# Decode attention, forward and backward: dK blocks alternate with the next pair's K blocks, and two V blocks take the place of dK blocks behind the sum of exponents

## The chip, the cores and the metric

The kernel runs on one core of a Trainium2 chip. Its engines work in parallel, each through its own queue in order: PE (TensorE, matmuls and transposes through the identity), DVE (VectorE), ACT (ScalarE), POOL (GpSimd) and SP (SyncE), which here issues the large transfers. The metric is the device time of one execution in microseconds. Before the change the median of three runs is 634.05 us (633.49 to 634.83).

## The reference

One query row per head, 32 heads, 8192 keys of 128 numbers, bf16. The kernel returns the attention output and the gradients of all three inputs:

```python
B, H, Sq, Skv, Dh = 1, 32, 1, 8192, 128
scores = jnp.einsum('bhqd,bhkd->bhqk', q, k) * Dh ** -0.5
attn = softmax(scores, axis=-1)                    # p
out = jnp.einsum('bhqk,bhkd->bhqd', attn, v)
# backward, for a given grad_out (do):
# dV = p (outer) do;  dp = V do;  ds = p * (dp - sum(p * dp)) * scale
# dK = ds (outer) q;  dq = ds K
```

K and V are read once (134 MB in all), and dK and dV, which are as large, are written once.

## The kernel before

Heads go in pairs: HP = 16 pairs, and the loop over t from 1 to 16 (L468) takes one pair a turn (pair 0 is done by `first()`; turn 16 only finishes). A pair's K and V are 4 MB each and lie in SBUF as 128 partitions by 128 rows by 128 numbers. There are three buffers for K and two for V. dK is written over K and dV over V, in place, and stored from there, so the load of pair t+2 waits until the store from the same buffer has landed.

The order of each engine's work is written out by hand (`tc.manual_schedule`, L100): an engine takes its instructions in the order of the Python calls. The work of a pair is cut in NB = 8 blocks of 16 rows:

- `k_block` (L197): DVE transposes a K block into one of three buffers named XK (L200), and PE adds four matmuls of it into the scores' bank `s_ps` (L208). XK is shared with the V blocks.
- `s_back`, `s_top` (L212, L217): DVE brings the scores back (`sT`, L215), takes the maximum, and PE spreads it (L223). `s_exp` (L225): DVE makes `nbias` (L230), ACT the exponents `e` and their sums (L233). `s_sum` (L237): PE adds the sums (L238).
- `p_of` (L247): DVE takes the reciprocal (L250); ACT makes `p_rep` (L252) and `win_p`, the weights for PE (L244).
- The V side. In turns 3 to 14 (`wide`, L257) half of V is transposed by DVE in four V blocks (`v_block`, L295, at L298), each read by four matmuls (`v_wide`, L302, at L310) into `dp_ps`. The other half goes through PE transposes (`v_part`: L273, copied by ACT at L279) and small matmuls (`v_scores`, L290). In the other turns all of V goes that second way.
- `contract` (L342): PE's products with V (`acc_p`) and, later, with K (`acc_ds`), both at L349. The first needs `win_p`, the second `win_ds`.
- `outer` (L367): DVE writes one block of dV (`"p"`) or dK (`"ds"`), at L371. `dk(a, b)` inside the loop does dK blocks a to b-1 of the pair in front, o = t-1, and issues the store of that dK when its last block (in the last two pairs: each half) is done.
- `v_back`, `pd_sum`, `ds_of` (L316 to L340): `dp_ps` comes back as `dpT` (L319), is multiplied and summed, and ds is made; ACT makes `win_ds` and `ds_rep`, which the dK blocks read.

A turn of 3 to 14 before the change goes, on DVE: dK blocks 0 to 3 of pair t-1; `sT`, maximum; dK block 4; `nbias`; dK blocks 5 and 6; reciprocal; V blocks 0 to 3; dK block 7; dV blocks 0 to 6 of pair t; `dpT`; dV block 7; ds; and the eight K blocks of pair t+1 in a row. On PE: the maximum's transpose, the sum, then four rounds of one `v_wide`, a quarter of `contract` for p and two `v_part`s, then `v_scores`, `contract` for ds, and the matmuls of the K blocks. SP's queue holds, turn by turn: the store of dK, the store of dV, the load of K, the load of V.

Of the kernel before, what the change touches and what calls it, by code (L numbers as in the profile page):

```python
# [15 lines left out]
NB = 8  # L16
# [11 lines left out]
def kernel(  # L28
# [14 lines left out]
    HP = H // 2  # L43
# [22 lines left out]
    psQ = ctx.enter_context(tc.tile_pool(name="psQ", bufs=1, space=PSUM))  # L66
    psM = ctx.enter_context(tc.tile_pool(name="psM", bufs=1, space=PSUM))

    st, acc = {}, {}
    k_in = [consts.tile([P, NT, D], BF16, name=f"K{i}") for i in range(K_BUFS)]  # L70
    v_in = [consts.tile([P, NT, D], BF16, name=f"V{i}") for i in range(V_BUFS)]
    Kt = {t: k_in[t % K_BUFS] for t in range(HP)}
# [2 lines left out]
    def rows_of(x, t, a, b):  # L75
        return x[0, 2 * t:2 * t + 2].rearrange("h s d -> (h s) d").rearrange("(p n) d -> p n d", p=P)[:, a:b, :]
# [120 lines left out]
    def k_block(t, c):  # L197
        x = st.setdefault(t, {})
        X = xkpool.tile([P, BN, NW, QD], F32, tag="XK", name="XK_sb")
        nc.vector.transpose(X[:], Kt[t][:, c * BN:(c + 1) * BN, :].rearrange("p n d -> p (n d)").bitcast(F32).rearrange(  # L200
            "p (n w j) -> p n w j", n=BN, w=NW))
        if c == 0:
            x["s"] = psS.tile([P, 512], F32, tag="s", name="s_ps")
        cols = X[:].rearrange("p n w i -> p (n w i)").bitcast(BF16).rearrange(
            "p (n w i e) -> p w e n i", n=BN, w=NW, e=2)
        for w in range(NW):
            for e2 in range(2):
                nc.tensor.matmul(x["s"][:], lhsT=q_win[:, 2 * w + e2, SL - 1 - c:SL - 1 - c + P],  # L208
                                 rhs=cols[:, w, e2], start=(c == 0 and w == 0 and e2 == 0),
                                 stop=(c == NB - 1 and w == NW - 1 and e2 == 1), skip_group_check=True)  # L210
# [6 lines left out]
    def s_top(t):  # L217
        x = st[t]
        mx = small.tile([P, 1], F32, tag="mx")
        nc.vector.reduce_max(mx[:], x["sT"][:, :, 0:NB], axis=AX.XY)  # L220
        top = small.tile([P, 1], F32, tag="top")
        nc.vector.tensor_scalar_mul(top[:], mx[:], scale)  # L222
        nc.tensor.transpose(x["m"][:, 128:256], top[:].to_broadcast([P, P]), ident_f[:])  # L223
# [13 lines left out]
    def s_sum(t, rs):  # L237
        nc.tensor.matmul(st[t]["m"][:, 0:1], lhsT=same[:], rhs=rs[:], start=True, stop=True, skip_group_check=True)  # L238
# [18 lines left out]
    def wide(t):  # L257
        return 3 <= t < HP - 1
# [22 lines left out]
    def v_scores(t, z):  # L281
        x = st[t]
        cols = x.pop(("XV", z)).rearrange("p m s -> p (m s)").bitcast(BF16).rearrange(
            "p (m s e) -> p e m s", s=P, e=2)
        if z == 0 and not wide(t):
            x["dp"] = psD.tile([P, 512], F32, tag="dp", name="dp_ps")
        at = SL - 2 - 2 * z
        for e2 in range(2):
            for b in range(NQ):
                nc.tensor.matmul(x["dp"][b * QD:(b + 1) * QD, :], lhsT=do_win[:, b // 2, e2, at:at + QD],  # L290
                                 rhs=cols[:, e2, :, b * QD:(b + 1) * QD],
                                 start=(not wide(t) and z == 0 and e2 == 0),
                                 stop=(z == (1 if wide(t) else NZ - 1) and e2 == 1), skip_group_check=True)

    def v_block(t, r):  # L295

        X = xkpool.tile([P, NM, NW, QD], F32, tag="XK", name="XV_blk")
        nc.vector.transpose(X[:], Vt[t][:].rearrange("p n d -> p (n d)").bitcast(F32).rearrange(  # L298
            "p (m r w j) -> p m r w j", r=SL, w=NW, j=QD)[:, :, SL // 2 + r])
        st[t]["XW", r] = X  # L300
# [66 lines left out]
    def outer(t, which, r):  # L367
        x = st[t]
        X, row = (Kt[t], 0) if which == "ds" else (Vt[t], 1)
        a, b = r * BN, (r + 1) * BN  # L370
        nc.vector.tensor_tensor(  # L371
            X[:, a:b, :].rearrange("p n (a b) -> p n a b", b=R),
            x[which][:, a:b, :].unsqueeze(2).to_broadcast([P, BN, D // R, R]),
            x["qd"][:, row, :].rearrange("p (a b) -> p a b", b=R).unsqueeze(1).to_broadcast([P, BN, D // R, R]),
            op=ALU.mult)

    def store(t, which, parts=1, last=None):
        X, dst = (Kt[t], out_2) if which == "ds" else (Vt[t], out_3)
        L = NT // parts
        for c in (range(parts) if last is None else (last,)):  # L380
            nc.sync.dma_start(rows_of(dst, t, c * L, (c + 1) * L), X[:, c * L:(c + 1) * L, :])
# [86 lines left out]
    for t in range(1, HP + 1):  # L468
        o = t - 1
        now = t < HP  # L470
        parts = 2 if o >= HP - 2 else 1

        def dk(a, b):
            for r in range(a, b):
                outer(o, "ds", r)
                if (r + 1) % (NB // parts) == 0:
                    store(o, "ds", parts, r * parts // NB)

        blocks = now and wide(t)
        if blocks:  # L480

            dk(0, 4)
            s_back(t)
            s_top(t)
            dk(4, 5)
            rs = s_exp(t)
            s_sum(t, rs)
            dk(5, NB - 1)
            p_of(t)
            for r in range(3):  # L490
                v_block(t, r)
            for i in range(4):
                v_wide(t, i)
                if i == 0:
                    v_block(t, 3)
                    dk(NB - 1, NB)
                contract(t, "p", i * NG // 4, (i + 1) * NG // 4)
                for z in range(2):
                    v_part(t, z * (NM // TB) + i)
                if i == 3:  # L500
                    for z in range(2):
                        v_scores(t, z)
                outer(t, "p", 2 * i)
                if i < 3:
                    outer(t, "p", 2 * i + 1)
            weights_do(t + 1)
            if wide(t + 1):
                weights_wide(t + 1)
        else:
            dk(0, 3)  # L510
            if now:
                v_part(t, 3)
                v_part(t, 4)
                s_back(t)
                s_top(t)
                v_scores(t, 0)
                v_part(t, 5)
                v_part(t, 6)
                rs = s_exp(t)
                for m in (7, 8, 9):  # L520
                    v_bank(t, m)
                s_sum(t, rs)
                v_copy(t, 7)
                v_copy(t, 8)
            dk(3, 4)
            if now:
                p_of(t)
                v_copy(t, 9)
                v_scores(t, 1)
                v_part(t, 10)  # L530
                v_part(t, 11)
                contract(t, "p")
                v_part(t, 12)
                v_part(t, 13)
                v_scores(t, 2)
                v_part(t, 14)
                v_part(t, 15)
                v_scores(t, 3)
                if t + 1 < HP:
                    weights_do(t + 1)  # L540
                    if wide(t + 1):
                        weights_wide(t + 1)
        if not now:
            dk(4, NB - 1)
            results()
            dk(NB - 1, NB)
            break
        fine, early = t == HP - 1, NB - 1 if blocks else 2
        if not blocks:
            dk(4, NB)  # L550
            outer(t, "p", 0)
            outer(t, "p", 1)
            if fine:
                store(t, "p", 4, 0)
        v_back(t)
        pd_sum(t)
        if t % ST == 0:
            gather(o, "ds")
        outer(t, "p", early)
        if blocks:  # L560
            store(t, "p")
        ds_of(t)
        contract(t, "ds")
        if t % ST == ST - 1:
            gather(t, "p")
        if t + 1 < HP:
            prepare(t + 1)
        else:
            gather(t, "ds")
        done = 0  # L570
        for r in range(early + 1, NB):
            outer(t, "p", r)
            if fine and r % 2:
                store(t, "p", 4, r // 2)
            if t + 1 < HP and t != 1:
                k_block(t + 1, done)
                done += 1
        if not fine and not blocks:
            store(t, "p")
        if t + 1 < HP:  # L580
            for c in range(done, NB):
                k_block(t + 1, c)
                if not wide(t + 1) and c > HALF:
                    v_part(t + 1, c - HALF - 1)
        if t + 2 < HP:
            weights_q(t + 2)
            load_k(t + 2)
            load_v(t + 2)
# [32 lines left out]
```

## Time and profile before

| | before |
|---|---|
| median of three runs | 634.05 us |
| the profiled execution | 634.35 us |
| its span | 632.5 us |
| mean granted clock of PE | 0.812 |
| busy: PE, DVE, ACT | 426.6, 550.5, 176.2 us |
| DMA, share of 16 engines, rate | 99.0%, 425 GB/s |
| DVE waiting for PE before a K block | 37.9 us |

The profile shows one execution. L200 is line 200 of the kernel, "DVE" or "PE" the engine. In the slices a digit is the busy share in tenths of one fortieth of the span, for PEclk the clock that PE was granted in tenths of full. The chain goes back from the last instruction to whatever released it, step by step, and gives shares of the span. A line of the waits reads: who waited <- for whom: microseconds in total, times, longest. In the order of time a line gives start, duration, engine, line, operation, tiles and, in brackets, the idle time before it and who ended it. In a table of stretches a line gives the stretch, its length, the busy time of PE, PE's weight loads, DVE, ACT and POOL with the number of instructions, the granted clock, the DMA share and GB/s.

### The profile page before, as it was taken

The page shows a single profiled execution, that of the slowest core. Times are in us where ns is not written, and L with a number is a line of the kernel's source. Part 1 is how long each engine was busy: PE and PEld are TensorE (multiplying, and loading weights), DVE is VectorE, ACT ScalarE, POOL GpSimd, SP SyncE. Part 2 cuts the span into 40 slices and gives each one's busy share as a digit, 9 for nine tenths or more (in the row PEclk, how much of TensorE's full clock was granted, in tenths as well). Part 3 has the DMA queues.
Part 4 walks back from the last instruction along what each step waited for, and adds up shares of the span by engine and source line. Part 5 has one row for each costly group of instructions (what it writes and reads, how often), then busy time and mean ns, then how long its engine had stood idle before and what let it go on. Part 6 is the DMA issues. An engine that isn't in the chain of part 4 may idle for free.

```text
span 632.5 us, 7251 instructions
## 1 busy us (share of the span) xinstructions
PE 426.6 (67%) x2876; PEld 207.7 (33%) x2876; DVE 550.5 (87%) x630; ACT 176.2 (28%) x439; POOL 9.2 (1%) x27
## 2 busy tenths in 40 slices
PE   5868686488475874758747587474875748757870
PEld 2635252144242421323323242231332314223540
DVE  8688987997988979899797997989979799798893
ACT  1616152041240322404124031240412304122530
POOL 2000000000000000000000000000000000000000
PEclk9989697787698776888868877687886878768965
DMA  8999999999999999999999999999999999999997
GB/s 361 434 418 433 431 430 430 433 432 430 431 430 430 434 424 435 428 435 432 434 443 430 429 432 432 428 431 432 431 428 431 430 431 432 430 432 432 411 407 310
DMA packets 11025, 268.92 MB, mean 425 GB/s; under 512 B 1392, under 2 KB 1392, under 8 KB 1392
## 3 DMA queue, kind: packets, MB, share of 16 engines
q1 hardware_dynamic: 10896, 268.46, 99.0%
q8 instruction: 22, 0.36, 0.2%
q14 instruction: 11, 0.09, 0.0%
q10 hardware_dynamic: 96, 0.02, 0.0%
HBM read 134.23 MB, written 134.23 MB: 424 GB/s over the span
## 4 chain that ended last, share of the span: by engine, by line
PE 41%; DVE 40%; issue 7%; ACT 6%; DMA 4%; DVEq 0%; ACTq 0%
DVE K L371 18%; PE T_ps L273 9%; PE dp_ps L310 9%; DVE XK_sb L200 9%; PE acc_ds L349 7%; PE acc_p L349 6%; PE s_ps L208 5%; DVE V L371 5%; DMA K<-in_k_dram 3%; PE dp_ps L290 3%; DVE XV_blk L298 2%; ACT XV_sb L279 2%; ACT win_ds L244 2%; DVE sT L215 2%; DVE dpT L319 1%
## 5 line engine op out<-in xcount | busy, mean ns | idle before, releaser
L200 DVE STREAM_TRANSPOSE XK_sb<-K 128x1024 f32<-128x1024 f32 x128 | 148.6, 1215 | 40.3 <-PE s_ps L208 37.9
L371 DVE TENSOR_TENSOR V<-p_rep,qd 128x2048 bf16<-128x2048 bf16 x128 | 150.8, 1219 | 7.6 <-PE T_ps L273 3.4
L371 DVE TENSOR_TENSOR K<-ds_rep,qd 128x2048 bf16<-128x2048 bf16 x128 | 149.2, 1211 | 0.5
L208 PE MATMUL s_ps<-XK_sb,q_win 128*128 128x512 bf16 x512 | 132.9, 404 | 9.9 <-DVE XK_sb L200 5.8
L279 ACT COPY XV_sb<-T_ps 128x512 f32<-128x512 f32 x144 | 78.2, 589 | 130.4 <-PE T_ps L273 130.3
L273 PE MATMUL T_ps<-ident_f,V 128*128 128x128 f32 x640 | 92.8, 293 | 0.1
L273 PEld LDWEIGHTS T_ps<-ident_f,V 128*128 128x128 f32 x640 | 75.3, 150 | 34.0 <-issue 26.6
L310 PE MATMUL dp_ps<-XV_blk,do_wide 128*128 128x512 bf16 x192 | 62.3, 454 | 31.2 <-DVE XV_blk L298 31.2
L208 PEld LDWEIGHTS <-q_win 128*128 128x128 bf16 x512 | 50.9, 102 | 85.0 <-issue 38.3
L349 PE MATMUL acc_ds<-K,win_ds 128*32 128x512 bf16 x512 | 52.9, 586 | 33.3 <-ACT win_ds L244 33.3
L298 DVE STREAM_TRANSPOSE XV_blk<-V 128x1024 f32<-128x1024 f32 x48 | 55.3, 1208 | 0.0
L223 PE MATMUL m_ps<-ident_f,top 128*128 128x128 f32 x16 | 6.7, 416 | 62.2 <-DVE top L222 62.2
L349 PE MATMUL acc_p<-V,win_p 128*32 128x512 bf16 x512 | 42.7, 428 | 1.6 <-ACT win_p L244 1.6
L310 PEld LDWEIGHTS <-do_wide 128*128 128x128 bf16 x192 | 19.9, 109 | 49.6 <-DVE XV_blk L298 32.2
L349 PEld LDWEIGHTS <-win_ds 128*32 128x32 bf16 x512 | 17.2, 130 | 56.1 <-ACT win_ds L244 31.2
L185 ACT COPY q_win<-q_blk 128x16 bf16<-128x16 bf16 x16 | 4.2, 261 | 108.7 <-PE s_ps L208 108.7
L233 ACT ACTIVATE e<-sT,nbias 128x128 f32<-128x128 f32 x16 | 8.2, 515 | 69.7 <-DVE nbias L230 69.7
L223 PEld LDWEIGHTS m_ps<-ident_f,top 128*128 128x128 f32 x16 | 2.7, 170 | 68.8 <-issue 62.2
L290 PE MATMUL dp_ps<-XV_sb,do_win 128*32 128x512 bf16 x288 | 20.8, 383 | 5.2 <-ACT XV_sb L279 5.0
L238 PE MATMUL m_ps<-rs,same 128*128 128x1 f32 x32 | 8.3, 327 | 18.1 <-ACT e L233 18.1
L244 ACT ACTIVATE win_ds<-ds,rinv_s 64x128 bf16<-64x128 f32 x32 | 12.8, 399 | 27.5 <-DVE ds L336 27.3
L328 PE MATMUL m_ps<-pd,same 128*128 128x1 f32 x32 | 6.1, 260 | 19.8 <-DVE m_ps L322 19.8
(68 smaller groups left out, 215.0 us busy)
## 6 DMA issues: line engine op xcount, KB each, us to landing
K<-in_k_dram SPq DMA_DIRECT2D x15, 4096.0 KB, 19.2
V<-in_v_dram SPq DMA_DIRECT2D x15, 4096.0 KB, 19.3
out_dram<-V SPq DMA_DIRECT2D x15, 4096.0 KB, 25.4
out_dram<-K SPq DMA_DIRECT2D x14, 4096.0 KB, 27.4
out_dram<-K SPq DMA_DIRECT2D x4, 2048.0 KB, 9.5
K<-in_k_dram SPq DMA_DIRECT2D x4, 1024.0 KB, 8.2
V<-in_v_dram SPq DMA_DIRECT2D x4, 1024.0 KB, 15.6
out_dram<-V SPq DMA_DIRECT2D x4, 1024.0 KB, 8.3
```

The costliest lines, as they stand in the source:

```text
L200: nc.vector.transpose(X[:], Kt[t][:, c * BN:(c + 1) * BN, :].rearrange("p n d -> p (n d)").bitcast(F32).rearrange("p (n w j) -> p n w j", ...
L208: nc.tensor.matmul(x["s"][:], lhsT=q_win[:, 2 * w + e2, SL - 1 - c:SL - 1 - c + P], rhs=cols[:, w, e2], start=(c == 0 and w == 0 and e2 == 0),
L215: nc.vector.transpose(x["sT"][:].rearrange("p n r -> p (n r)"), x.pop("s")[:])
L223: nc.tensor.transpose(x["m"][:, 128:256], top[:].to_broadcast([P, P]), ident_f[:])
L244: nc.scalar.activation(win[which][a:b, :, at + 4 * s:at + 4 * s + 4], src[a:b].rearrange("p (g j) -> p g j", j=4), ACT.Copy, scale=1.0 if ...
L273: nc.tensor.transpose(T_ps[:, j, :], words[:, at * P:(at + 1) * P], ident_f[:])
L279: nc.scalar.copy(x["XV", z][:, i * TB:(i + 1) * TB, :], x.pop(("T", m))[:])
L290: nc.tensor.matmul(x["dp"][b * QD:(b + 1) * QD, :], lhsT=do_win[:, b // 2, e2, at:at + QD], rhs=cols[:, e2, :, b * QD:(b + 1) * QD], start ...
L298: nc.vector.transpose(X[:], Vt[t][:].rearrange("p n d -> p (n d)").bitcast(F32).rearrange("p (m r w j) -> p m r w j", r=SL, w=NW, j=QD)[:, ...
L310: nc.tensor.matmul(st[t]["dp"][:], lhsT=do_wide[:, 2 * w + e2, at:at + P], rhs=cols[:, w, e2], start=(r == 0 and w == 0 and e2 == 0), stop ...
L349: nc.tensor.matmul(acc[which][b * QD:(b + 1) * QD, :], lhsT=win[which][:, g, at:at + QD], rhs=X[:, 4 * g:4 * g + 4, :].rearrange("p n d -> ...
L371: nc.vector.tensor_tensor(X[:, a:b, :].rearrange("p n (a b) -> p n a b", b=R), x[which][:, a:b, :].unsqueeze(2).to_broadcast([P, BN, D // ...
```

## The change

`dk` now takes only the block up to which to go, and remembers in `wrote` how far the pair's dK is written, so a pair's dK blocks can be begun in the turn before. In the turns of 3 to 14, dK blocks 0 to 3 of pair t (0 to 2 in turn 14) are placed behind K blocks 2 to 5 (2 to 4) of pair t+1. In the next turn dK blocks 4 and 5 stand ahead of `sT`, block 6 behind the maximum, and behind `nbias` and the sum come V blocks 0 and 1, where dK blocks 5 and 6 were; then the reciprocal and `p_of`, V blocks 2 and 3, and dK block 7 as before. Turn 3 has no dK block placed ahead and writes six before `sT`. In turn 15 dK block 3, with the store of the first half, stands behind the maximum, and block 4 ahead of the reciprocal; three more follow it. Nothing changes in what is computed, nor in the order of PE, ACT, POOL and SP.

```diff
-    st, acc = {}, {}
+    st, acc, wrote = {}, {}, {}
...
-        parts = 2 if o >= HP - 2 else 1
-
-        def dk(a, b):
-            for r in range(a, b):
+
+        def dk(b, o=o):
+
+            parts = 2 if o >= HP - 2 else 1
+            for r in range(wrote.get(o, 0), b):
                 outer(o, "ds", r)
                 if (r + 1) % (NB // parts) == 0:
                     store(o, "ds", parts, r * parts // NB)
+                wrote[o] = r + 1
...
-            dk(0, 4)
+            dk(6)
             s_back(t)
             s_top(t)
-            dk(4, 5)
+            dk(NB - 1)
             rs = s_exp(t)
             s_sum(t, rs)
-            dk(5, NB - 1)
+            v_block(t, 0)
+            v_block(t, 1)
             p_of(t)
-            for r in range(3):
-                v_block(t, r)
+            v_block(t, 2)
             for i in range(4):
                 v_wide(t, i)
                 if i == 0:
                     v_block(t, 3)
-                    dk(NB - 1, NB)
+                    dk(NB)
...
-            dk(0, 3)
+            dk(3)
             if now:
                 v_part(t, 3)
                 v_part(t, 4)
                 s_back(t)
                 s_top(t)
+                if t == HP - 1:
+                    dk(4)
                 v_scores(t, 0)
...
-            dk(3, 4)
+            dk(5 if t == HP - 1 else 4)
...
-            dk(4, NB - 1)
+            dk(NB - 1)
             results()
-            dk(NB - 1, NB)
+            dk(NB)
...
             for c in range(done, NB):
                 k_block(t + 1, c)
+                if blocks and 2 <= c < (6 if wide(t + 1) else 5):
+                    dk(c - 1, t)
                 if not wide(t + 1) and c > HALF:
                     v_part(t + 1, c - HALF - 1)
```

More of the change, by code (lines that the diff above doesn't have):

```diff
@@ L549 @@
         if not blocks:
-            dk(4, NB)
+            dk(NB)
             outer(t, "p", 0)
```

## The prediction

> **What bounds the kernel now.** I read the page first (share of the engines, the slices, the queues, the chain), then the waits, then one middle turn in order of time, then the granted clock in stretches.
>
> ```profile
> span 632.5 us, 7251 instructions
> ...
> PE 426.6 (67%) x2876; PEld 207.7 (33%) x2876; DVE 550.5 (87%) x630; ACT 176.2 (28%) x439; POOL 9.2 (1%) x27
> ...
> PEclk9989697787698776888868877687886878768965
> DMA  8999999999999999999999999999999999999997
> ...
> q1 hardware_dynamic: 10896, 268.46, 99.0%
> ...
> PE 41%; DVE 40%; issue 7%; ACT 6%; DMA 4%; DVEq 0%; ACTq 0%
> ```
>
> Two things could set the pace. The DMA engines are full in nearly every slice. Yet the chain that ended last holds 4% of DMA and is a relay of PE and DVE. The waits decide between them:
>
> ```profile
> DVE XK_sb L200 <- PE s_ps L208: 37.9, 17, 4.6
> ...
> PE dp_ps L310 <- DVE XV_blk L298: 31.2, 12, 2.6
> ...
> DVE XK_sb L200 <- DMA K<-in_k_dram: 2.4, 1, 2.4
> ```
>
> Compute waited for a load once, in turn 2. Later K loads land early: the one issued at 357.57 takes 19.2 us by the list of issues (376.8) and is first read at 381.83. So the compute chain paces the turns (39.2 us each, by sT of turns 4 and 11 at 162.31 and 436.62) and the transfers keep up with about 5 us in hand. A longer chain is paid in full; a shorter one only until that is used.
>
> Now turn 9 (start, duration, engine, line):
>
> ```profile
> 348.41 5.75 DVE L200 STREAM_TRANSPOSE XK_sb<-K 128x1024 f32<-128x1024 f32 x5 [2.34 <-PE s_ps L208]
> ...
> 358.58 0.71 DVE L215 STREAM_TRANSPOSE sT<-s_ps 128x512 f32<-128x512 f32 x1
> ...
> 361.91 0.58 PE L238 MATMUL m_ps<-rs,same 128*128 128x1 f32 x2 [1.51 <-ACT e L233]
> 363.73 0.17 DVE L250 RECIPROCAL rinv<-m_ps 128x1 f32<-128x1 f32 x1
> ...
> 364.81 0.64 ACT L244 ACTIVATE win_p<-p_rep 64x128 bf16<-64x128 bf16 x2
> ...
> 365.10 1.89 PE L310 MATMUL dp_ps<-XV_blk,do_wide 128*128 128x512 bf16 x4 [2.60 <-DVE XV_blk L298]
> 366.91 1.04 PE L349 MATMUL acc_p<-V,win_p 128*32 128x512 bf16 x8
> ...
> 379.27 0.72 DVE L319 STREAM_TRANSPOSE dpT<-dp_ps 128x512 f32<-128x512 f32 x1 [0.37 <-PE dp_ps L290]
> ```
>
> From sT (L215) to the first V matmul (L310) it is 6.52 us, from there to dpT (L319) 14.17. In that second part PE works without a gap and DVE waits for it (0.37 us before dpT), so **PE is the bound between the first V block and dpT**. How long PE takes depends on its clock. Stretches: length, PE busy, the others, granted clock, DMA:
>
> ```profile
> 104.88:108.29 3.41, 3.02 (x8) 0.92 (x7) 3.41 (x4) 0.00 (x0) 0.00 (x0) 0.50 1.05 447
> 108.29:111.70 3.41, 1.57 (x7) 0.55 (x6) 3.41 (x4) 0.00 (x0) 0.00 (x0) 1.00 1.05 452
> 111.70:115.12 3.42, 2.88 (x8) 0.94 (x7) 3.42 (x4) 0.00 (x0) 0.00 (x0) 0.50 0.89 383
> ...
> 364.29:367.71 3.42, 2.62 (x12) 0.56 (x12) 3.42 (x4) 1.26 (x4) 0.00 (x0) 0.50 1.00 431
> 365.10:371.12 6.02, 6.02 (x24) 2.70 (x24) 6.02 (x6) 1.71 (x5) 0.00 (x0) 0.50 1.01 435
> ...
> 443.13:446.21 3.08, 3.08 (x14) 0.85 (x15) 3.08 (x3) 0.54 (x3) 0.00 (x0) 0.50 1.11 479
> ```
>
> The clock moves in steps of 3.41 us, and a step's activity decides the next one. After 88% and 84% busy it is full, after 46% half, after 76% (364.29) it stays half. So waking PE takes one whole step with at most about 0.54 us idle (84%). Each of the twelve V stages starts at half clock. From the first L310 until full clock it takes W, and until dpT D: W 3.08 gives D 12.73 (turn 11), W 6.02 gives 14.17 (turn 9). I call the slope 0.49 us per us; the mean over turns 3 to 14 is W 4.4, D 13.36.
>
> **The change, part by part.** The span is 632.5 us, the profiled execution 634.35, which is 0.3 above the median 634.05. No instruction is added; DVE alone is reordered. PE, ACT, POOL and SP keep their order, so each DMA is issued behind the same ones, and the K store still follows dK block 7, behind the same DVE work. One block is 1.15 us of DVE (L200 1215 ns, L371 1211, L298 1208; five in 5.75 back to back).
>
> *Alternating K and dK (turns 4 to 14).* dK block 0 goes behind the third K block, where DVE waits for PE (2.3 to 4.6 us in these turns): hidden, saving 1.15. Its own inputs are ready: ds_rep comes about 1.5 us after the first K block starts, and the matmuls of L349 that read this block's rows are the first four. But six dK blocks now stand before sT instead of four: +2.30. Net +1.15 on sT. The K blocks now come every 2.3 us for 1.03 us of PE at full clock: 45%, which by the row of 46% makes the clock fall. At half clock the last two K blocks, which still come back to back, need 3.5 us of PE, against two dK blocks behind them: sT waits 0 to 0.5 us. I take +0.25.
>
> *Two V blocks behind the sum of exponents.* V block 0 now follows nbias, so the first L310 stands 4.02 us behind sT instead of 6.52 (nbias to V start 0.03, V start to L310 1.28, both as in turn 9): −2.50. But the reciprocal now stands behind V block 1, at sT + 5.05, and win_p hangs on it. By the rows above L349 can start 1.87 us after the reciprocal starts (365.45, when win_p ends, plus 0.15 of hand-over, less 363.73), so at sT + 6.92. PE is through with its first four L310 1.81 us after their start, at sT + 5.83. So PE, in order, gets **a hole of 1.1 us that was not there: +1.1**. Queued behind it are all further V matmuls and transposes, and DVE's V outers wait for those.
>
> *What the hole does to the clock.* It exceeds 0.54 us, so no step that contains it wakes PE. The waking step must start at 2.4 us or later behind the first L310 (1.81 + 1.1 − 0.54); it ends 3.41 us on at 5.8, or, by its place, up to 9.2: mean 7.5 for 4.4. Without the hole itself, in which nothing runs slowly, that is 2.0 us more at half clock: 0.49 × 2.0 = +1.0. Bounds: −0.5 if W stays 4.4 in spite of the hole, +1.8 at 9.2 in every turn. I take +1.0; the row that failed at 76% had only 0.80 us idle, so it is nearest.
>
> Sum per turn: 1.15 + 0.25 − 2.50 + 1.1 + 1.0 = **+1.0**, eleven times +11.0. DVE covers none of it: its order behind dpT is unchanged.
>
> *Turn 3* has no alternated K blocks before it: +2.30 on sT, −2.50, +1.1, +1.1 (its W was 4.15): **+2.0**.
>
> *Turn 15.* Two dK blocks (1.15 each beyond the hidden one) now stand before the last K blocks, whose matmuls alternate on PE with v_parts. K block 5 ends at 589.2 instead of 586.9; PE then needs three K blocks and two v_parts (3 × 1.03 + 2 × 0.60 = 4.3), so sT moves from 592.5 to about 593.7: +1.2. With the clock fallen before (45% again) up to 2.2 more. The dK blocks that leave the stage behind sT give nothing back before dpT, where DVE waits 0.90 us for PE; from dpT on DVE sets the end. I take **+2.2**, ends +1.2 and +3.4.
>
> Total +15.2: 634.35 + 15.2 − 0.3 ≈ **649 us**. With every turn at its best step (W 5.8) it is +4 to +5; near the bad end +23: own range 640 to 657.
>
> [...]
>
> **Rivals.**
> 1. *Faster: the hole does not keep the clock down* (W 4.4 as before). Then a turn is 1.15 + 0.25 − 2.50 + 1.1 − 0.5 = −0.5, eleven of them −5.5, turn 3 +0.5, turn 15 +2.2: −2.8. The transfers cap it: from 595 to 630 the stretches moved 13.5 MB, at the 430 GB/s of the slices 31.4 us instead of 33.9, so at most about −2.5. Time 631.5. The hinge is W: turns break even when it is near 5.4. For it: only 37.9 us of waits on PE are visible, and DVE fills part of them. Against: four rows of the clock.
> 2. *The transfers set the pace* (99% busy), compute is slack, and nothing moves: 634. For it: every slice reads 9. Against: one wait for a load, 5 us in hand. It decides only if a turn lengthens by less than the chain shows.
> 3. *Slower still*: the step always falls late and the last K blocks always run at half clock: +2.05 per turn, turns 3 and 15 +2.9 and +3.4: 663.
>
> **How the numbers follow.** Forecast 0.60, rival 1 0.20, rival 2 0.12, rival 3 0.08. About 0.2% (1.3 us) is what a measurement of this kernel can tell from none. Faster 0.20, same 0.12, slower 0.68. The range holds the forecast's own 640 to 657, reaches down over rival 2, and to the near edge of rival 1: 631.3 to 657.
>
> **What would show it.** Right: the wait of XK_sb for s_ps falls from 37.9 us by about 12; a new wait of acc_p (L349) for win_p of about 1.1 us in each of 12 turns, some 13 us in all where it was 1.6; V outers wait longer for T_ps; sT to the first L310 reads 4.0; D is 14.6 to 16.3; the mean granted clock falls below 0.81; DMA below 99%. Wrong: no wait at L349 (then win_p came sooner or the first L310 later), or the wait with D near 14, which would mean that the clock rose through it.

## The result, and the profile after

The changed kernel takes 651.95 us (649.65 to 653.06, five runs) against 634.05 before: the ratio is 1.0276, with an interval from 1.0262 to 1.029. It is slower by 2.8%. Its profiled execution took 653.06 us, 18.7 more than the one of before; its span is 18.7 longer too. One run among the experiments, 652.42 us with 0.43 us of the hole filled, lies 2.2% above the fastest of its kernel and is left out there as slow.

The page of the changed kernel, the lines that answer to those shown of before:

```profile
span 651.3 us, 7263 instructions
...
PE 456.8 (70%) x2876; PEld 216.4 (33%) x2876; DVE 551.9 (85%) x630; ACT 176.9 (27%) x439; POOL 9.3 (1%) x27
...
PEclk9979687787689777888578977788857896778985
DMA  8999999999999999999999999999999999899598
...
q1 hardware_dynamic: 10896, 268.46, 97.2%
```

DVE does the same work in the same busy time (551.9 us, 550.5 before). PE does the same work in 30 us more (456.8 for 426.6): its mean granted clock fell from 0.812 to 0.797. The transfers, at 99.0% before, are at 97.2% and now have gaps. The waits of the changed kernel:

```profile
DVE XK_sb L200 <- PE s_ps L208: 31.8, 14, 4.4
DVE V L371 <- PE T_ps L273: 27.4, 24, 1.8
...
PE acc_p L349 <- ACT win_p L244: 14.4, 16, 1.1
```

The second and third were 3.4 and 1.6 us before. Turn 8 of the changed kernel, in order of time:

```profile
329.73 0.71 DVE L215 STREAM_TRANSPOSE sT<-s_ps 128x512 f32<-128x512 f32 x1
...
333.05 0.59 PE L238 MATMUL m_ps<-rs,same 128*128 128x1 f32 x2 [1.66 <-ACT e L233]
333.78 1.89 PE L310 MATMUL dp_ps<-XV_blk,do_wide 128*128 128x512 bf16 x4
334.88 0.17 DVE L250 RECIPROCAL rinv<-m_ps 128x1 f32<-128x1 f32 x1
...
335.96 0.64 ACT L244 ACTIVATE win_p<-p_rep 64x128 bf16<-64x128 bf16 x2
336.74 1.04 PE L349 MATMUL acc_p<-V,win_p 128*32 128x512 bf16 x8 [1.07 <-ACT win_p L244]
...
343.49 6.10 DVE L371 TENSOR_TENSOR V<-p_rep,qd 128x2048 bf16<-128x2048 bf16 x5 [1.78 <-PE T_ps L273]
...
349.94 0.72 DVE L319 STREAM_TRANSPOSE dpT<-dp_ps 128x512 f32<-128x512 f32 x1 [0.35 <-PE dp_ps L290]
```

The first L310 stands 4.05 us behind sT (6.51 before), and behind it the hole: L349 waits 1.07 us for win_p, whose reciprocal stands behind V block 1. From the first L310 to dpT it is 16.16 us, where the slowest turn before had 14.17. The stretches of this stage (length, PE busy, the others, granted clock) show what the hole does to the clock:

```profile
333.78:342.93 9.15, 8.08 (x35) 3.51 (x36) 6.98 (x7) 2.72 (x6) 0.00 (x0) 0.50 1.02 440
342.93:349.94 7.01, 6.73 (x63) 3.59 (x61) 5.95 (x5) 3.22 (x6) 0.31 (x1) 1.00 0.99 425
```

PE runs at half clock for 9.15 us (W) after the first L310; in turn 8 of before it was 4.91.

### The profile page after: what moved, and what is told of

Its sections match the earlier page's. It is cut to its first block, busy times and chain, and to the rows that moved or that the text cites. A ratio compares the mean times of both kernels' runs of the same rounds, so it can differ in the third digit from the quotient of the medians.

```text
span 651.3 us, 7263 instructions
## 1 busy us (share of the span) xinstructions
PE 456.8 (70%) x2876; PEld 216.4 (33%) x2876; DVE 551.9 (85%) x630; ACT 176.9 (27%) x439; POOL 9.3 (1%) x27
## 3 DMA queue, kind: packets, MB, share of 16 engines
q1 hardware_dynamic: 10896, 268.46, 97.2%
## 4 chain that ended last, share of the span: by engine, by line
PE 39%; DVE 38%; ACT 8%; issue 8%; DMA 5%; DVEq 0%; SPq 0%; ACTq 0%
DVE K L371 12%; DVE XK_sb L200 11%; PE T_ps L273 10%; PE acc_ds L349 7%; PE acc_p L349 6%; PE dp_ps L310 6%; PE s_ps L208 5%; DVE V L371 5%; DMA K<-in_k_dram 5%; DVE XV_blk L298 4%; PE dp_ps L290 3%; ACT XV_sb L279 2%; ACT p_rep L252 2%; ACT win_ds L244 2%; ACT win_p L244 1%
## 5 line engine op out<-in xcount | busy, mean ns | idle before, releaser
L200 DVE STREAM_TRANSPOSE XK_sb<-K 128x1024 f32<-128x1024 f32 x128 | 152.1, 1222 | 32.8 <-PE s_ps L208 31.8
L208 PE MATMUL s_ps<-XK_sb,q_win 128*128 128x512 bf16 x512 | 144.8, 429 | 42.2 <-DVE XK_sb L200 40.5
L273 PE MATMUL T_ps<-ident_f,V 128*128 128x128 f32 x640 | 98.9, 306 | 0.1
L208 PEld LDWEIGHTS <-q_win 128*128 128x128 bf16 x512 | 53.1, 106 | 126.1 <-issue 86.7
L273 PEld LDWEIGHTS T_ps<-ident_f,V 128*128 128x128 f32 x640 | 80.4, 157 | 37.3 <-issue 29.9
L349 PE MATMUL acc_ds<-K,win_ds 128*32 128x512 bf16 x512 | 56.5, 621 | 33.3 <-ACT win_ds L244 33.3
L310 PE MATMUL dp_ps<-XV_blk,do_wide 128*128 128x512 bf16 x192 | 69.5, 497 | 2.1 <-DVE XV_blk L298 0.7
L349 PE MATMUL acc_p<-V,win_p 128*32 128x512 bf16 x512 | 46.1, 457 | 14.4 <-ACT win_p L244 14.4
L349 PEld LDWEIGHTS <-win_ds 128*32 128x32 bf16 x512 | 17.8, 139 | 60.0 <-ACT win_ds L244 31.2
L310 PEld LDWEIGHTS <-do_wide 128*128 128x128 bf16 x192 | 21.5, 118 | 23.5 <-issue 13.5
L223 PE MATMUL m_ps<-ident_f,top 128*128 128x128 f32 x16 | 5.0, 311 | 34.0 <-DVE top L222 33.9
L349 PEld LDWEIGHTS <-win_p 128*32 128x32 bf16 x512 | 9.7, 98 | 47.3 <-issue 45.4
```

Of the source, the lines that this page charges most:

```text
L273: nc.tensor.transpose(T_ps[:, j, :], words[:, at * P:(at + 1) * P], ident_f[:])
L310: nc.tensor.matmul(st[t]["dp"][:], lhsT=do_wide[:, 2 * w + e2, at:at + P], rhs=cols[:, w, e2], start=(r == 0 and w == 0 and e2 == 0), stop ...
L349: nc.tensor.matmul(acc[which][b * QD:(b + 1) * QD, :], lhsT=win[which][:, g, at:at + QD], rhs=X[:, 4 * g:4 * g + 4, :].rearrange("p n d -> ...
```

## The experiments

Theory H, the prediction's: the hole ahead of L349, and the half clock that it prolongs, make the loss. Rival A: the alternation makes it, by the dK blocks put before sT and by K blocks that PE does at half clock.

**Closing the hole.** The reciprocal and `p_of` move ahead of V block 1; nothing else changes.

```diff
             v_block(t, 0)
-            v_block(t, 1)
             p_of(t)
+            v_block(t, 1)
             v_block(t, 2)
```

> The changed kernel with one move: the reciprocal and what hangs on it stand behind V block 0 instead of behind V block 1, so V block 1 comes after the reciprocal. Theory H (the hole ahead of L349 and the clock behind it make the loss): win_p is ready about 1.9 us after the first L310 instead of 2.96, the hole shrinks from 1.1 us to about 0.1, W falls from 8.3 to near 4.4 and D from 15.8 to about 13.4; with sT to L310 still at 4.05, a turn is 0.5 to 1.2 us shorter than before and the time 629 to 637 us. Rival A (the alternation makes the loss: more dK blocks before sT, and K blocks at half clock): the time stays at 648 to 653 us, whatever the hole does.

Measured: 634.31 us, ratio 1.0005 (0.9996 to 1.0015) to the kernel before. The whole loss is gone, with the alternation in place, so rival A falls. From the first L310 to L349 it is 1.84 us instead of 2.96. Between the first L310 and dpT PE is at half clock for 4.3 us in the mean of turns 3 to 14 (8.2 with the change, 4.4 before), and mean D is 13.3. The faster times within the range that I gave did not come, although DVE's last block now ends at 616.4 instead of 622.5. The waits of this kernel and its last stretches say what holds it:

```profile
DVE XK_sb L200 <- DMA K<-in_k_dram: 18.8, 9, 3.3
```

```profile
626.00:627.00 1.00, 0.00 (x0) 0.00 (x0) 0.00 (x0) 0.00 (x0) 0.00 (x0) 0.50 0.54 230
...
629.00:630.00 1.00, 0.00 (x0) 0.00 (x0) 0.00 (x0) 0.00 (x0) 0.00 (x0) 0.50 0.15 66
630.00:631.00 1.00, 0.00 (x0) 0.00 (x0) 0.00 (x0) 0.00 (x0) 0.00 (x0) 0.50 0.04 16
```

The last two figures of a line are DMA share and GB/s. Compute now waits for loads nine times where it waited once: it has run into the transfers. And the mean share of the sixteen DMA engines falls from 0.54 to 0.04 over five microseconds; when each single one ends is not shown. The kernel before ends with the last two of these lines, figure for figure, although its DVE ends 6.1 us later. So I estimate, from the times of this kernel and the one before and from these lines, that about 634 us is what the transfers in this order allow (no run has the transfers by themselves); the kernel before then already stood at it.

**The V order alone.** The two lines that put dK blocks among the K blocks are taken out.

```diff
                 k_block(t + 1, c)
-                if blocks and 2 <= c < (6 if wide(t + 1) else 5):
-                    dk(c - 1, t)
```

> The changed kernel without the alternation: no dK block among the K blocks, six of them before sT, the V blocks behind the sum as changed. Theory H: the hole and the slow clock are there in all twelve turns as in turn 3 of the changed kernel; per turn +2.3 before sT, -2.5, +1.1, +1.2 = +2.1, so 652 to 664 us. Rival A: without alternated K blocks the K stage is as before, +2.3 and -2.5 cancel, and the time is 632 to 638 us.

Measured: 661.76 us, ratio 1.0439 (1.0423 to 1.0454), inside H's range. The hole is there (acc_p waits 14.5 us for win_p in all), and without the alternation it is dearer: two more dK blocks before sT cost 2.4 us a turn (12.60 us from the fourth K block to sT, 10.19 before), and none fills DVE's wait in the K stage (45.6 us of waits for s_ps). With the V order as changed, the alternation saves 9.8 us.

**The alternation alone.** The order behind the sum is put back.

```diff
+            p_of(t)
             v_block(t, 0)
             v_block(t, 1)
-            p_of(t)
             v_block(t, 2)
```

> The changed kernel with the order behind the sum put back: reciprocal first, then the V blocks; the alternation stays. DVE then waits about 1.3 us for the sum ahead of the reciprocal, and the first L310 stands 5.5 us behind sT. Theory H: no hole, W near 4.4, D near 13.4; per turn +1.8 (K stage) - 1.0 = +0.8 at most, so 634 to 645 us. Rival A: 648 to 655 us.

Measured: 634.78 us, ratio 1.0013 (1.0004 to 1.0022). DVE waits for the sum ahead of the reciprocal (19.4 us in all), the first L310 stands 5.26 us behind sT, there is no hole, and mean W is 4.41 and D 13.36, for 4.38 and 13.36 before. In this kernel's time the alternation alone costs at most 0.2%, but compute ends 3.7 us later than before (DVE's last block at 626.2): 1.3 us of it comes in turn 3 and 2.15 in turn 15, and the transfers hide most of it.

**Filling the hole.** Three matmuls with weights of zero, added to `dp_ps`, occupy PE in the hole. The order is that of the changed kernel, and L349 starts as late as there.

```diff
                 if i == 0:
+                    warm(t)
                     v_block(t, 3)
                     dk(NB)
...
+    def warm(t):
+        cols = st[t]["XW", 1][:].rearrange("p n w i -> p (n w i)").bitcast(BF16).rearrange(
+            "p (n w i e) -> p w e n i", n=NM, w=NW, e=2)
+        for m in (NM, NM, NM // 2):
+            nc.tensor.matmul(st[t]["dp"][:, 0:m * QD], lhsT=zero[:], rhs=cols[:, 0, 0, 0:m],
+                             start=False, stop=False, skip_group_check=True)
```

> The changed kernel with 1.1 us of extra matmuls (weights of zero, added to dp_ps, so they change no sum) on PE in the hole, between the first four L310 and the first L349. The hole's time is still lost, but PE is not idle in it. Theory H with both parts (hole 1.1 us, clock 1.2 us): W falls from 8.3 to near 4.4, D from 15.8 to about 14.5, a turn is 1.2 us shorter than with the change, the time 635 to 646 us. If the clock plays no part and only the 1.1 us are lost, or if rival A holds: D stays near 15.8 and the time at 648 to 653 us.

Measured: 634.31 us, ratio 1.0002 (0.9993 to 1.0012): 17.6 us faster than the changed kernel, by work that serves nothing, and just below the range that I gave H. Its turn 8, from the first L310 to dpT:

```profile
321.53:327.30 5.77, 5.75 (x24) 2.78 (x25) 4.80 (x6) 2.15 (x5) 0.00 (x0) 0.50 1.04 449
327.30:336.15 8.85, 8.57 (x77) 4.34 (x75) 8.12 (x7) 3.81 (x8) 0.31 (x1) 1.00 0.97 418
```

The half clock lasts 5.77 us instead of 9.15. From the first L310 to L349 it is still 2.97 us, but mean D is 13.9 for 15.8, and from dpT of turn 3 to dpT of turn 14 it is 426.2 us, where the changed kernel took 453.0 and the kernel before 433.8. So of the two parts of theory H the lost 1.1 us could be borne (the V blocks that come 2.5 us sooner outweigh it, and compute waits for a K load seven times), and **the clock is what makes the loss**.

**How little is enough.** The same with fewer matmuls: 0.64 us of them (one of 512 columns and one of 256), and 0.43 us (one of 512).

```diff
-        for m in (NM, NM, NM // 2):
+        for m in (NM, NM // 2):
```

> The same with 0.64 us of extra matmuls; about 0.45 us of the hole stay idle, less than the 0.54 us that woke PE before. Theory H: W falls to 3 to 6.4, D to about 14, the time to 633 to 637 us, as with the hole filled. If it is not idleness but the late start of the first L349 that costs: 648 to 653 us.

Measured: 634.07 us, ratio 1.0002 (0.9992 to 1.0011). With 0.44 us of the hole idle PE woke as before: 4.3 us at half clock between the first L310 and dpT, D 13.9.

```diff
-        for m in (NM, NM, NM // 2):
+        for m in (NM,):
```

> The changed kernel with 0.43 us of extra matmuls (weights of zero) in the hole; some 0.65 us of the 1.1 us stay idle. Between the steps that did not wake PE (0.80 us idle) and those that did (0.54): if the limit lies below 0.65 us, W stays at 6.8 to 9.2 and the time at 645 to 653 us; if above, W falls to 3 to 6.4 and the time to 633 to 637 us.

Measured: 642.23 us (638.46 to 644.44, three runs), ratio 1.0121 (1.0078 to 1.0164): neither branch, but both in turn. dpT of turns 5, 9 and 13:

```profile
222.47 0.72 DVE L328 STREAM_TRANSPOSE dpT<-dp_ps 128x512 f32<-128x512 f32 x1 [0.35 <-PE dp_ps L292]
...
380.39 0.72 DVE L328 STREAM_TRANSPOSE dpT<-dp_ps 128x512 f32<-128x512 f32 x1 [0.35 <-PE dp_ps L292]
...
544.23 0.72 DVE L328 STREAM_TRANSPOSE dpT<-dp_ps 128x512 f32<-128x512 f32 x1 [0.34 <-PE dp_ps L292]
```

The first four of these turns took 157.92 us, the next four 163.84, which is the changed kernel's own pace: W is 3.5 and 3.7 in turns 5 and 6, and 9.1, 8.2, 8.6, 6.8, turn for turn as with the change, from turn 8 on. Steps with 0.65 us idle went both ways: the one that starts at 208.99 woke PE, those that start at 325.04 (PE is at half clock from 322.74 to 331.86) and 366.00 did not. So did steps with 0.64 us idle in the changed kernel: the one from 271.25 to 274.66 (half clock, 2.77 of 3.41 us busy) is followed by one at full clock, the one from 336.10 to 339.51 (half clock, 2.77 busy) by another at half. From these steps I estimate that the limit on idleness lay near 0.65 us in 3.41 there, between the 0.54 and 0.80 that the prediction read.

**Whole steps.** The 163.84 led to the next question. dpT of turns 8 and 12 before, with the change, and with the V order alone, in three fences:

```profile
338.87 0.72 DVE L319 STREAM_TRANSPOSE dpT<-dp_ps 128x512 f32<-128x512 f32 x1 [0.36 <-PE dp_ps L290]
495.89 0.72 DVE L319 STREAM_TRANSPOSE dpT<-dp_ps 128x512 f32<-128x512 f32 x1 [0.36 <-PE dp_ps L290]
```

```profile
349.94 0.72 DVE L319 STREAM_TRANSPOSE dpT<-dp_ps 128x512 f32<-128x512 f32 x1 [0.35 <-PE dp_ps L290]
513.78 0.72 DVE L319 STREAM_TRANSPOSE dpT<-dp_ps 128x512 f32<-128x512 f32 x1 [0.35 <-PE dp_ps L290]
```

```profile
353.63 0.72 DVE L319 STREAM_TRANSPOSE dpT<-dp_ps 128x512 f32<-128x512 f32 x1 [0.34 <-PE dp_ps L290]
520.91 0.72 DVE L319 STREAM_TRANSPOSE dpT<-dp_ps 128x512 f32<-128x512 f32 x1 [0.35 <-PE dp_ps L290]
```

157.02, 163.84 and 167.28 us for four turns (the small products of `gather` come round every four) are 46.0, 48.0 and 49.0 steps of the clock of 3.413 us (the changes of the clock lie whole multiples of it apart: 167 of them from 36.61 to 606.64 in the kernel before, 176 from 35.73 to 636.47 with the change); the alternation alone has 46.0. Theory L: the turns lock onto the clock's steps. A turn that starts late by some time wakes that much earlier in its own time, and D gives back 0.49 of it (the slope between turns 11 and 9 of before), until four turns fit a whole number. To test it, the kernel before got a small DVE reduction (279 ns) that nobody reads, ahead of sT in turns 3 to 14, once and twice.

```diff
             dk(0, 4)
+            for j in range(1):
+                nc.vector.reduce_max(pad[:, j:j + 1], same[:], axis=AX.X)
             s_back(t)
```

> The kernel before with one small DVE reduction (128x128, about 0.29 us) whose result nobody reads, put ahead of sT in turns 3 to 14. In the runs so far four turns take a whole number of clock steps of 3.413 us: 46.0 before (157.01 us), 48.0 with the change (163.83), 49.0 with the V order alone, 46.0 with the alternation alone. Theory L (the turns lock onto the steps of PE's clock): four turns take 46.0 or 47.0 steps (157.0 or 160.4 us), never 46.35; since W was already at its least (3.05) in one turn of four before, 47 is likelier: 642 to 646 us, else 634 to 636. Rival (delays add): four turns take 158.2 us, 46.35 steps, and the time is 637 to 639 us.

> The same with two such reductions, 0.58 us a turn. Theory L: again a whole number of steps, 47.0 where one reduction gives 47.0, so the time is within 3 us of that of one reduction. Rival (delays add): four turns take 159.3 us, 46.7 steps, and the time is 640 to 643 us, 3.5 us above one reduction.

Measured: once, 635.44 us (633.56 to 637.34), ratio 1.0020 (1.0007 to 1.0033); twice, 640.51 us (638.02 to 644.14), ratio 1.0106 (1.0069 to 1.0144). The totals do not decide for L: the first lies in the less likely of its two ranges and below the rival's, but the second lies where the rival had it, and 5 us above the first, not within 3. The paces, in the one profiled execution of each, do. dpT of turns 8 and 12 with two reductions:

```profile
347.86 0.72 DVE L320 STREAM_TRANSPOSE dpT<-dp_ps 128x512 f32<-128x512 f32 x1 [0.35 <-PE dp_ps L291]
508.31 0.72 DVE L320 STREAM_TRANSPOSE dpT<-dp_ps 128x512 f32<-128x512 f32 x1 [0.37 <-PE dp_ps L291]
```

160.45 us, 47.0 steps, where added delays would give 159.3; from turn 4 on four turns come to 161.5 and then 160.4 to 160.6 throughout. With one reduction they come to 160.4 to 160.5 from turns 4, 5 and 6, and to 156.8 to 157.0 from turns 8, 9 and 10: it fell from 47 steps to 46. So these paces are whole steps, as L has them; that a late turn is drawn back to them by waking earlier in its own time is argued from the 0.49, not shown, and so is that the runs of one kernel differ by how many turns they spend at each pace. Where the hole is closed or filled, four turns from turn 4 on take 44.95 to 46.0 steps, with waits for loads among them.

## Why the prediction was right, and where its steps were off

The forecast was 649 us, slower, by a hole ahead of L349 and the clock behind it; the runs show that cause. Step by step, means of turns 4 to 14 from the two traces:

- *K stage.* From the first K block to sT +1.15 was forecast, with 0.25 more for a wait of sT. It grew by 1.78 (16.69 to 18.47). From the fourth K block on it is the forecast +1.13, and sT waited for nothing. The other +0.65 lies ahead of the fourth K block (6.50 to 7.15 behind the first): I held that start fixed, but it waits for PE's first K matmuls, and PE was at half clock for 6.6 us of that stretch a turn, 4.5 before. That is why the wait of XK_sb for s_ps fell by 6.1 us only, half of what I named, although dK block 0 stands in it. My reading that a step with little idle time wakes PE is too simple there. Two steps ahead of turn 8's sT:

```profile
312.20:315.61 3.41, 3.41 (x28) 2.03 (x20) 1.83 (x2) 0.00 (x0) 0.00 (x0) 0.50 1.07 461
315.61:319.02 3.41, 3.16 (x10) 1.28 (x10) 0.60 (x1) 0.54 (x2) 0.00 (x0) 0.50 1.02 442
```

PE is busy throughout the first and but for 0.25 us in the second, and the step behind them is still at half clock. They hold the end of `contract`, the small products of `gather` and the first K matmuls; why they did not wake PE stays open. In the kernel before, too, the steps from 101.47 (2.87 of 3.41 us busy) and 145.84 (3.41 busy) are each followed by one at half clock.

- *V blocks earlier:* −2.50 forecast, −2.46 measured. *Hole:* +1.1 forecast, +1.14 measured (1.82 to 2.96).
- *Clock:* +1.0 forecast, with W 7.5. Measured: W 8.3, D 15.79 less 13.37 less the hole, +1.28. The range of W, 5.8 to 9.2, held (6.8 to 9.15), but it was not spread evenly, as I had taken it: the turns repeat four values.
- *A turn:* +1.0 forecast, +1.74 measured, so +19.2 for eleven. *Turn 3:* +2.0 and +1.7 (dpT at 142.96 for 141.29).
- *Turn 15:* +2.2 forecast, +0.25 measured (dpT from 20.85 us late to 21.10). PE stayed at full clock there (1.00 from 609.00 to 613.57), and its three K blocks and two v_parts took 3.6 us (609.89 to 613.53), not 4.3, because each overlaps the one before it by 0.16 to 0.17 us. With the alternation alone the clock did fall there (half from 591.12 to 594.53), and turn 15 grew by the size that was forecast, 2.15 us.
- *Behind the last store:* nothing forecast, −2.4 measured. The last store is issued 21.1 us later (643.63 for 622.53), but the queue ahead of it is shorter (a store of half a dK lands 6.6 us behind its issue in the median, 9.5 before): the span ends 7.6 us on instead of 10.0.

The sum, 1.67 + 19.18 + 0.25 − 2.38 = 18.7, is the difference of the spans. So the mechanism and its parts held. That the size came near is partly luck: the term of a turn was too small by 0.74, 8 us over eleven turns, and turn 15 and the transfers at the end gave back over 4 of them. The forecast's own range was also added up loosely: its lower end, 640, lies above the 638 to 639 that its +4 to +5 give.

Of the rivals, the first (the clock rises through the hole) is refuted by W, and the third is nearly what a turn did (+1.74 of its +2.05), without its end. The second, that the transfers set the time, is wrong for the changed kernel and right for those whose hole is closed or filled. The cap of rival 1, 631.5 us, was wrong: it took the mean rate over sixteen engines up to the end (and 33.9 us for stretches of 35), but three kernels with compute to spare all stop at 634.1 to 634.3; over the last five microseconds the share falls from 0.54 to 0.04 with the hole closed, and from 0.65 to 0.04 with it filled by three matmuls.

Idle time counted at both clocks. With PE still at half clock, 1.1 us of idleness in the step cost all that was lost; and at full clock the step from 108.29 to 111.70 of the kernel before, 1.57 of 3.41 us busy and with 1.23 us as its longest gap, is followed by one at half clock.

## What to carry to other kernels

When work is moved forward on one engine, look at what the next engine in line needs second, not only first: here PE got its first operands 2.5 us sooner and then waited for the weights. At the start of a matmul stage that runs at half clock, look for gaps of PE (here 0.44 us did no harm, 0.65 did in some turns, 1.0 to 1.1 in all); moving one reciprocal by one instruction, or filling the gap with useless matmuls, gave back 18 us. And before hoping for a gain, see where a kernel with compute to spare would stop: those of this case stopped at 634.1 to 634.3 us, where this one already was.

## What the runs showed of the hardware that I had not expected

- This loop kept to whole steps of the clock: four turns took 46.0, 47.0, 48.0 or 49.0 steps of 3.413 us, in six kernels whose own work differs by amounts that are no multiples of it. Among these a pace changed by whole steps: one over four turns is 0.85 us a turn, 10 us over twelve turns. The times did not: the added reductions, 3.3 and 6.7 us of work, made the kernel before 1.5 and 6.5 us slower.
- Busy time by the profile did not alone decide whether PE woke: with 0.44 us of the hole idle it woke, but a step without any idle time, at 312.20 in the changed kernel (3.41 us busy), did not wake it.
- With 0.43 us of the hole filled, one kernel shows two paces in one execution (157.9, then 163.8 us for four turns). Its three runs lie between 638.46 and 644.44 us, where ten with 0.64 us filled lie between 633.80 and 634.30.
- Useless PE work was worth its time here: three matmuls of weights zero in each of twelve turns made the changed kernel 17.6 us faster.
- With the hole closed, where DVE's last block ends at 616.4, the mean share of the sixteen DMA engines falls over some 5 us (0.54 at 626 to 0.04 at 630) before the end. How this is spread over the single engines, and why it falls, is not shown.
